# Moving weight casts and small vector work in a fused attention and star-ReLU kernel

## The chip, the cores and the metric

The kernel runs on one core of a Trainium2 chip. The metric is the device time of one execution in microseconds (us). Before the change it is 718.2 us, the median of three runs (718.13 to 718.25). The profile is of one execution of 718.1 us, in which the first and the last instruction are 716.3 us apart, at a granted TensorE clock of 0.997.

Engines are called as the profile calls them: PE is TensorE (PEld its weight loads), ACT is ScalarE, DVE is VectorE, POOL is GpSimd, SP is SyncE. POOL and SP issue transfers here (as does ACT at the start and the end).

## The reference, cut to what matters

There are two parts. The first is an attention across channels, for each of four batches of 6080 rows and 256 channels; the second is a feed-forward layer with 2048 hidden features over all 24320 rows.

```python
def _attn_ref(q, k, v, tau):
    qn = q / (np.linalg.norm(q, axis=1, keepdims=True) + 1e-06)
    kn = k / (np.linalg.norm(k, axis=1, keepdims=True) + 1e-06)
    s = kn.transpose(0, 2, 1) @ qn / tau        # 256 x 256 for each batch
    s = s - s.max(-1, keepdims=True)
    a = np.exp(s)
    a /= a.sum(-1, keepdims=True) + 1e-09
    return (v @ a).astype(np.float32)

def _moe_ref(x, w_in, w_out, s, b):             # x: the attention's output
    h = x @ w_in
    r = np.maximum(h, 0.0)
    g = s * (r * r) + b
    return (g @ w_out).astype(np.float32)
```

## The kernel before

The kernel folds the small matrix `a` into `w_in` once for a batch (`wa`), so that v times `wa` gives h at once. The rows are worked on in 48 groups of at most 512 (the last has 256). Each group has 16 **steps**, numbered through the program (step 16 is the first of group 1); in each step PE computes one block of 128 of the 2048 features (`mm1`). A pair of steps fills one of two PSUM tiles, which ACT reads out with a relu; squares of the results are taken by ACT or DVE.

The second product, g times `w_out`, is done one group later. In group 0 and the last group it is done plainly with `w_out16`. In all other groups it is done with seven products of half size instead of eight. For that DVE forms four sums of quarters of g (`S[1]` to `S[4]`), and w_out has to be combined once into `T1`, `T2`, `T3` and `N4`. The products are accumulated in three PSUM halves X, Y and Z, and DVE reads results out between them:

```python
products = [
    ("X", G(0, 0), W[:, 0, :, lo], p1),      # p1: DVE reads X into u1
    ("Z", lambda: S[1], T1, p5),             # p5: DVE reads Z into u5
    ("X", lambda: S[2], T2, p6),             # p6: DVE reads X into u2
    ("Y", G(1, 0), W[:, 1, :, lo], p2),
    ("X", lambda: S[3], T3, p7),
    ("Z", lambda: S[4], W[:, 1, :, hi], p3),
    ("X", G(1, 1), N4, p4),
]
# each product: 8 blocks x 2 matmuls of 128 columns; 7 of the 112 matmuls in each step,
# from step 3 of the next group on
```

So group 1's products begin at step 35. The third, which reads T2, takes the matmuls 32 to 47 (steps 39 to 41), the fifth, which reads T3, the matmuls 64 to 79 (steps 44 to 46). T2 and T3 are made in four pieces of two blocks each.

w_out is loaded in float32 in four pieces (`w_pieces`) and then worked on between the steps:

```python
def combine_w(i, k):                 # all on DVE, two pieces at a time
    for n in (2 * k, 2 * k + 1):
        for p in (2 * i, 2 * i + 1):
            ...
            if n == 0:   po(nc.vector.tensor_sub(T1[:, part, :], B12, B11))
            elif n == 1: po(nc.vector.tensor_sub(B12, B22, B12))      # what T3 is cast from
            elif n == 2: po(nc.vector.tensor_add(B11, B11, B12))      # what T2 is cast from
            else:        po(nc.vector.tensor_sub(N4[:, part, :], B21, B11))

def cast_w_out(i):                   # piece 0 on DVE, the others on ACT
    ...

def cast_w(T, i):
    w = w_pieces[i].rearrange("p (i h) c -> p h i c", h=2)
    po(nc.scalar.copy(out=T[:, ts(i, 2), :], in_=w[:, 0, :, :P] if T is T2 else w[:, 0, :, P:]))

CO = (7, 14, 18, 24)      # steps of cast_w_out
CW = (17, 20, 25, 27)     # steps of combine_w
CT = (32, 34, 36, 38)     # steps of cast_w for T2; for T3 six steps later
```

`po` keeps the order of the program on each engine. Work put on a step with `at_step` comes after the step's matmuls, relus, squares and sums. The pieces of w_out lie in the pool of eight buffers that the loads of q and k use too.

While a batch is worked on, the matrix and the norms of the next batch are prepared. Its q and k come in 12 chunks of 512 rows. For each chunk PE accumulates q by k (`s_ps`), and the squares for the norms are taken and folded into one block of rows:

```python
def norm_ops(self, c):
    # ops in this order, for batches 1 to 3:
    #   squares of k (ACT), squares of q (DVE), fold 4 -> 2 (DVE), fold 2 -> 1 (DVE),
    #   for chunks 1 to 10: a POOL transfer that adds the result to the first chunk's
    ...

def norm_step(gr=gr, c=c, sc=sc):    # sc: the step of the chunk's first matmuls
    ops = gr.norm_ops(c)
    for i, f in enumerate(ops):
        at_step(int(sc) + 2 + 1 + i * 3, f)
```

In batch 1, chunk 0 has sc = 26 and chunk 1 has 32.75.

The order of a step, with the squares of g and the sums S:

```python
SQUARES = {3: (0, 1, nc.scalar), 5: (1, 2, nc.scalar), 8: (2, 4, nc.vector),
           12: (4, 6, nc.vector)}
SUMS = {2: 1, 3: 2, 6: 3, 10: 4}

for s in range(NS + FT):
    g, m = divmod(s, FT)
    if g < NG:
        mm1(g, m)
    ...                                # seven matmuls of the products, and their p1 to p7
    if g < NG and m % 2 == 1:
        relu(g, m // 2)                # ACT
    ...
    if g < NG and g not in plain and m in SQUARES:
        square(g, *SQUARES[m])
    ...
    elif m == 0 and 0 < g and g - 1 not in plain:
        square(g - 1, 6, 8, nc.vector)
    elif 0 < g and g - 1 not in plain and m in SUMS:
        sums_of(g - 1, SUMS[m])        # DVE
    for f in side.pop(s, []):          # what at_step has put here
        f()
```

Of the kernel before, what the change touches and what calls it, by code (L numbers as in the profile page):

```python
# [17 lines left out]
def kernel(  # L18
# [12 lines left out]
    nc = tc.nc  # L31
    P = 128
# [14 lines left out]
    FT = Dff // P  # L47
    TG = 512
    NG = (NT + TG - 1) // TG
# [6 lines left out]
    def po(ins):  # L56

        tc.keep_in_program_order(ins)
        return ins
# [29 lines left out]
    T1, T2, T3, N4 = (wpool.tile([P, NP, P], FP16, name=n) for n in ("T1", "T2", "T3", "N4"))  # L89
# [287 lines left out]
    def group(g):  # L377
        t0 = g * TG
        return t0, min(TG, NT - t0) // P
# [3 lines left out]
    def load_v(g):  # L383
        t0, nj = group(g)
        v16 = vpool.tile([P, TG // P, C], FP16, tag="v16", name="v16")
        po(nc.gpsimd.dma_start(  # L386
            out=v16[:, :nj, :],
            in_=v_flat[t0 : t0 + nj * P, :].rearrange("(p j) c -> p j c", j=nj)))
        v_tiles[g] = v16

    def transpose_v(g):
        _, nj = group(g)
        v16 = v_tiles.pop(g)
        vT_ps = ps_o.tile([P, CH, TG], FP16, tag="o_ps", name="vT_ps")
        for j in range(nj):
            for ch in range(CH):
                po(nc.tensor.transpose(vT_ps[:, ch, ts(j, P)], v16[:, j, ts(ch, P)], ident16))
        vT = vtpool.tile([P, CH, TG], FP16, tag="vT", name="vT")
        po(nc.vector.tensor_copy(out=vT[:, :, : nj * P], in_=vT_ps[:, :, : nj * P]))
        vT_tiles[g] = vT  # L400

    def crossbar_v(g):

        _, nj = group(g)
        v16 = v_tiles.pop(g)
        vT = vtpool.tile([P, CH, TG], FP16, tag="vT", name="vT")
        for j in range(nj):
            po(nc.sync.dma_start_transpose(out=vT[:, :, ts(j, P)], in_=v16[:, j, :]))
        vT_tiles[g] = vT
# [74 lines left out]
    for c in range(NCH0 - NLATE):  # L484
        ops = g0.norm_ops(c)
# [3 lines left out]
        if c == NCH0 - NLATE - 1:  # L489
            ops, last_sum = ops[:-1], ops[-1]  # L490
# [4 lines left out]
    ops = {c: g0.norm_ops(c) for c in late}  # L495
# [40 lines left out]
    def combine_w(i, k):  # L536

        for n in (2 * k, 2 * k + 1):
            for p in (2 * i, 2 * i + 1):
                w = w_pieces[p].rearrange("p (i h) c -> p h i c", h=2)  # L540
                B11, B12 = w[:, 0, :, :P], w[:, 0, :, P:]
                B21, B22 = w[:, 1, :, :P], w[:, 1, :, P:]
                part = ts(p, 2)
                if n == 0:
                    po(nc.vector.tensor_sub(T1[:, part, :], B12, B11))
                elif n == 1:
                    po(nc.vector.tensor_sub(B12, B22, B12))
                elif n == 2:
                    po(nc.vector.tensor_add(B11, B11, B12))
                else:  # L550
                    po(nc.vector.tensor_sub(N4[:, part, :], B21, B11))

    def cast_w_out(i):
        if i == 0:
            po(nc.vector.tensor_copy(out=w_out16[:, ts(i, 4), :], in_=w_pieces[i]))
        else:
            po(nc.scalar.copy(out=w_out16[:, ts(i, 4), :], in_=w_pieces[i]))

    def cast_w(T, i):
        w = w_pieces[i].rearrange("p (i h) c -> p h i c", h=2)  # L560
        po(nc.scalar.copy(out=T[:, ts(i, 2), :], in_=w[:, 0, :, :P] if T is T2 else w[:, 0, :, P:]))


    side, early = {}, {}
# [1 line left out]
    def at_step(s, f):  # L566
        side.setdefault(int(s), []).append(f)
# [5 lines left out]
    for i, f in enumerate(folds):  # L573
        early.setdefault(FOLDS[i], []).append(f)
    at_step(14, lambda: po(nc.vector.tensor_scalar_mul(
        out=s_out, in0=s_bc, scalar1=1.0 / (LAM * LAM))))

    RC = (13, 16, 19, 21, 23)
    CO = (7, 14, 18, 24)
    CW = (17, 20, 25, 27)  # L580
    CT = (32, 34, 36, 38)
    for i in range(NPIECE):
        at_step(CO[i], lambda i=i: cast_w_out(i))
    for i in range(NPIECE + 1):
        at_step(RC[i], lambda i=i: rowconst_sum(i))
    at_step(30, rowconst_mm)
    for i in range(NPIECE):
        at_step(CW[i], lambda i=i: combine_w(i // 2, i % 2))
        at_step(CT[i], lambda i=i: cast_w(T2, i))
        at_step(CT[i] + 6, lambda i=i: cast_w(T3, i))  # L590
    for g in range(NG):
        if g >= 3:
            at_step(max(g - 4, 0) * FT + 2, lambda g=g: load_v(g))
        if g >= 1:
            if g == 1:
                at_step(12, lambda g=g: transpose_v(g))
            else:
                at_step((g - 2) * FT + 6, lambda g=g: crossbar_v(g))
    for b in range(1, B):
        gr = grams[b]  # L600
        w0 = first_group[b - 1] * FT + (26 if b == 1 else 6)
        w1 = first_group[b] * FT - 3
        NCH = len(gr.chunks)
        fin_len = 54
        span = (w1 - fin_len) - w0 - 12
        n = NCH * JC
        for c in range(NCH):
            sc = w0 + span * c * JC / n
            at_step(max(3, sc - 16), lambda gr=gr, c=c: gr.load(c))
            if c == 0:  # L610
                at_step(sc, gr.start)
            for j in range(JC):
                at_step(w0 + span * (c * JC + j) / n, lambda gr=gr, c=c, j=j: gr.mm(c, j))

            def norm_step(gr=gr, c=c, sc=sc):
                ops = gr.norm_ops(c)
                for i, f in enumerate(ops):
                    at_step(int(sc) + 2 + 1 + i * 3, f)
            at_step(sc + 1, norm_step)

        def fin_step(gr=gr, s=w1 - fin_len):
            ops = gr.finish_ops()
            for i, f in enumerate(ops):
                at_step(int(s) + 1 + (FIN[i] if i < len(FIN) else FIN[-1] + 3 * (i - len(FIN) + 1)), f)
        at_step(w1 - fin_len - 12, fin_step)
# [37 lines left out]
    def relu(g, i):  # L663
        n = group(g)[1] * P
        if i % 2 == 0:
            r_tiles[g, i // 2] = rpool.tile([P, 2, 2, TG], FP16, tag="r16", name="r16")
        r16 = r_tiles[g, i // 2]
        po(nc.scalar.activation(out=r16[:, :, i % 2, :n], in_=h_tiles.pop((g, i))[:, :, :n],  # L668
                                func=AF.Relu))

    def square(g, i0, i1, engine):

        n = group(g)[1] * P
        if i0 == 0:
            g_tiles[g] = gpool.tile([P, 2, NP, TG], FP16, tag="g16", name="g16")
        src = r_tiles[g, i0 // 2][:, :, i0 % 2 : i0 % 2 + i1 - i0, :n]
        dst = g_tiles[g][:, :, i0:i1, :n]
        if engine is nc.scalar:
            po(nc.scalar.activation(out=dst, in_=src, func=AF.Square))  # L679
        else:  # L680
            po(nc.vector.tensor_mul(dst, src, src))  # L681
# [79 lines left out]
    def seven_items(g):  # L761
# [56 lines left out]
        for n, (name, a, w, after) in enumerate(products):  # L818
            for i in range(NP):
# [15 lines left out]
    plain = {0, NG - 1}  # L835
    PLAG = {0: 11, NG - 1: 5}

    SQUARES = {3: (0, 1, nc.scalar), 5: (1, 2, nc.scalar), 8: (2, 4, nc.vector),
               12: (4, 6, nc.vector)}
# [10 lines left out]
# [4 lines that stand above are left out]
        for f in early.pop(s, []):  # L854
            f()

        if m == SHIFT and 0 < g and g - 1 not in plain:
            items = seven_items(g - 1)
            work.append((items, 8 if g == NG - 1 else 7))
        if work:  # L860
            items, n = work[0]
            for f in items[:n]:
                f()
            del items[:n]
            if not items:
                work.pop(0)
        for gp in plain:
            for mp in range(FT):
                if s == gp * FT + PLAG[gp] + (mp * 4 // 3 if gp == 0 else mp):
                    plain_mm2(gp, mp)  # L870
        if g < NG and m % 2 == 1:
            relu(g, m // 2)
            if g in plain:
                late = g > 0 and m // 2 % 2 == 0
                square(g, m // 2, m // 2 + 1, nc.scalar if late else nc.vector)
        if g < NG and g not in plain and m in SQUARES:
            square(g, *SQUARES[m])
        if g == NG - 1 and m in LAST:
            LAST[m]()
        elif m == 0 and 0 < g and g - 1 not in plain:  # L880
            square(g - 1, 6, 8, nc.vector)
        elif 0 < g and g - 1 not in plain and m in SUMS:
            sums_of(g - 1, SUMS[m])
        for f in side.pop(s, []):
            f()
# [34 lines left out]
```

## Time and profile before

| | us |
|---|---|
| time, median of 3 | 718.2 |
| span of the profiled run | 716.3 |
| PE busy in the span | 696.8 |
| DVE busy | 624.0 |
| ACT busy | 544.7 |
| POOL busy | 110.8 |
| ACT casts of T2 and T3 (8, mean of one) | 0.412 |
| ACT casts of w_out (3, mean of one) | 1.045 |
| ACT squares of a chunk's k (median of one) | 1.04 |
| DVE square of a chunk's q (mean of one, near 60 us) | 0.683 |
| DVE folds (mean of one, first and second) | 0.682 and 0.416 |

Durations of neighbouring instructions of one engine overlap in the profile, so the table's durations cannot simply be added: the distance from one start to the next is what an instruction takes of its engine. Ends of matmuls are modelled; their starts are recorded. In the profile's rows, "out<-in" gives the names of what is written and read, L with a number is the line of the kernel, x with a number counts instructions, and what stands in brackets is idle time of the engine before the instruction, with what ended it.

### The profile page before, as it was taken

Reading aid. Unit: us, or ns where it says so; the run is one execution under the profiler, and the core shown is the slowest. Engines: PE = TensorE matmul, PEld = TensorE weight load, DVE = VectorE, ACT = ScalarE, POOL = GpSimd, SP = SyncE. Lnnn points to the kernel's source line nnn. Section 1 sums busy time; section 2 is a strip of 40 time slices with the busy share of each in tenths; the row PEclk is TensorE's granted clock in tenths of the full one; section 3 lists DMA queues with packets and bytes.
Section 4 is the critical chain, followed back from the end, with each engine's and each line's share of the span. In section 5 each row is a group of like instructions: output and inputs, shape, how many; then the busy total and the mean of one; then the engine's idle time right before and its main releaser. Section 6 shows DMA issues by size and latency. Waiting matters only on the chain.

```text
span 716.3 us, 17491 instructions
## 1 busy us (share of the span) xinstructions
PE 696.8 (97%) x7421; PEld 503.6 (70%) x7421; DVE 624.0 (87%) x877; ACT 544.7 (76%) x592; POOL 110.8 (15%) x189
## 2 busy tenths in 40 slices
PE   4699999999999999999999999999999999999998
PEld 2456777776677777777677777777668777777777
DVE  4889999988789989998889899998887888888886
ACT  5779877787777777778777778777877777777874
POOL 4532332102101222101010222110000000000000
PEclk9999999999999999999999999999999999999999
DMA  9999999636565978444672887843323333321201
GB/s 236 207 259 167 165 174 136 122 89 124 111 122 109 135 134 144 112 89 95 138 146 52 145 137 125 153 90 77 98 63 75 94 70 75 97 60 46 82 31 75
DMA packets 87454, 83.47 MB, mean 117 GB/s; under 512 B 56304, under 2 KB 62256, under 8 KB 87376
## 3 DMA queue, kind: packets, MB, share of 16 engines
q0 software_dynamic: 26608, 43.40, 37.7%
q1 hardware_dynamic: 60192, 37.64, 22.0%
q8 instruction: 58, 0.95, 0.6%
q10 hardware_dynamic: 576, 1.31, 0.5%
q14 instruction: 20, 0.16, 0.1%
HBM read 78.91 MB, written 24.90 MB: 145 GB/s over the span
## 4 chain that ended last, share of the span: by engine, by line
PE 93%; DMA 3%; DVE 2%; ACT 2%; issue 0%; ACTq 0%; DVEq 0%
PE h_ps L658 45%; PE o_ps L826 40%; PE s_ps L148 4%; PE wa_ps L327 2%; DMA qk<-in_k_dram 1%; DMA raw<-in_q_dram 1%; ACT sq L177 1%; PE o_ps L730 1%; DVE f L191 1%; PE o_ps L704 0%; ACT r L668 0%; ACT r L269 0%; DVE sq L174 0%; PE n_ps L244 0%; DVE o_sb L686 0%
## 5 line engine op out<-in xcount | busy, mean ns | idle before, releaser
L668 ACT ACTIVATE r<-h_ps 128x1024 f16<-128x1024 f32 (+1 forms) x384 | 388.4, 1013 | 151.8 <-PE h_ps L658 148.1
L658 PE MATMUL h_ps<-vT,wa 128*128 128x512 f16 (+7 forms) x1632 | 452.2, 364 | 0.6 <-ACT wa L320 0.5
L826 PEld LDWEIGHTS <-S 128*128 128x128 f16 x2944 | 198.0, 98 | 84.8 <-issue 0.2
L826 PEld LDWEIGHTS <-g 128*128 128x128 f16 x2208 | 155.1, 98 | 74.1
L681 DVE TENSOR_TENSOR g<-r 128x2048 f16<-128x2048 f16 (+2 forms) x150 | 174.6, 1164 | 14.0 <-ACT r L668 13.6
L826 PE MATMUL o_ps<-T,S 128*128 128x128 f16 x2208 | 183.3, 219 | 0.1
L658 PEld LDWEIGHTS <-wa 128*128 128x128 f16 x1632 | 135.8, 98 | 20.6 <-ACT wa L320 0.8
L826 PE MATMUL o_ps<-w_out,g 128*128 128x128 f16 x1472 | 134.2, 219 | 0.2 <-DVE u L686 0.2
L686 DVE SCALAR_TENSOR_TENSOR o_sb<-o_ps,s_out,u 128x256 f32<-128x256 f32 x138 | 66.4, 481 | 50.9 <-PE o_ps L826 48.8
L679 ACT ACTIVATE g<-r 128x1024 f16<-128x1024 f16 (+1 forms) x97 | 100.4, 1035 | 0.2
L148 PE MATMUL s_ps<-qk 128*128 128x256 f16 (+1 forms) x384 | 71.7, 288 | 14.2 <-ACT qk L139 9.0
L386 POOL DMA_DIRECT2D v<-in_v_dram x48 | 31.0, 648 | 263.6 <-DMA vT<-v 187.0
L686 DVE SCALAR_TENSOR_TENSOR u<-o_ps,s_out,rowconst 128x256 f32<-128x256 f32 x138 | 65.8, 477 | 0.0
L826 PE MATMUL o_ps<-w_out,S 128*128 128x128 f16 x736 | 63.5, 219 | 0.0
L826 PE MATMUL o_ps<-N,g 128*128 128x128 f16 x736 | 63.4, 219 | 0.0
L207 POOL DMA_DIRECT2D f<-f x30 | 26.3, 876 | 224.3 <-DVE f L191 183.1
L755 DVE TENSOR_TENSOR S<-S,g 128x2048 f16<-128x2048 f16 (+1 forms) x47 | 56.4, 1201 | 1.3
L177 ACT ACTIVATE sq<-qk 128x1024 f16<-128x1024 f16 (+2 forms) x53 | 54.5, 1041 | 3.9 <-DMA qk<-in_k_dram 2.3
L753 DVE TENSOR_TENSOR S<-g 128x2048 f16<-128x2048 f16 (+1 forms) x47 | 56.0, 1192 | 0.0
L757 DVE TENSOR_TENSOR S<-g 128x2048 f16<-128x2048 f16 x46 | 55.9, 1215 | 0.0
L759 DVE TENSOR_TENSOR S<-g,S 128x2048 f16<-128x2048 f16 x46 | 55.8, 1214 | 0.0
L148 PEld LDWEIGHTS <-qk 128*128 128x128 f16 (+1 forms) x384 | 33.0, 103 | 20.8 <-ACT qk L139 9.5
(83 smaller groups left out, 313.9 us busy)
## 6 DMA issues: line engine op xcount, KB each, us to landing
out_dram<-o_sb SPq DMA_DIRECT2D x42, 512.0 KB, 2.9
v<-in_v_dram POOLq DMA_DIRECT2D x47, 256.0 KB, 4.9
qk<-in_k_dram POOLq DMA_DIRECT2D x42, 256.0 KB, 7.0
qk<-in_q_dram POOLq DMA_DIRECT2D x42, 256.0 KB, 7.7
f<-f POOLq DMA_DIRECT2D x30, 128.0 KB, 3.1
vT<-v SPq DMA_TRANSPOSE x182, 3.0
out_dram<-o_sb SPq DMA_DIRECT2D x10, 256.0 KB, 5.4
w<-in_moe_w_out_dram POOLq DMA_DIRECT2D x4, 512.0 KB, 10.1
```

Of the source, the lines that this page charges most:

```text
L148: po(nc.tensor.matmul(self.s_ps[:, ch, :], qc[:np_, j, ts(ch, P)], kc[:np_, j, :], start=(c == 0 and j == 0 and ch == 0), stop=(c == len(s ...
L177: po(nc.scalar.activation(out=st["sq"][:np_, a, js, :], in_=(qc, kc)[a][:np_, js, :], func=AF.Square))
L658: po(nc.tensor.matmul(dst, wa[:, ci, ts(m, P)], src, start=(ci == 0), stop=(ci == CH - 1), skip_group_check=True))
L668: po(nc.scalar.activation(out=r16[:, :, i % 2, :n], in_=h_tiles.pop((g, i))[:, :, :n], func=AF.Relu))
L679: po(nc.scalar.activation(out=dst, in_=src, func=AF.Square))
L681: po(nc.vector.tensor_mul(dst, src, src))
L686: po(nc.vector.scalar_tensor_tensor(out=dst, in0=src, scalar=s_out, op0=ALU.mult, in1=add, op1=ALU.add))
L753: po(nc.vector.tensor_add(T[1], A21, A22))
L755: po(nc.vector.tensor_sub(T[2], T[1], A11))
L757: po(nc.vector.tensor_sub(T[3], A11, A21))
L759: po(nc.vector.tensor_sub(T[4], A12, T[2]))
L826: po(nc.tensor.matmul(st[name][:, j, :], a()[:, i, ts(j, P)], w[:, i, :], start=first, stop=last, skip_group_check=True))
```

## The change: what it does and what it is for

- **w_out's casts (CO)**: the casts of pieces 1, 2 and 3 into `w_out16` are put on steps 12, 14 and 18.
- **T2 and T3 (cast_w, CT)**: the eight casts are no longer ACT instructions, but transfers from SBUF to SBUF, issued by GpSimd, that convert float32 to float16 on the way. T2's pieces are put on steps 22, 23, 28 and 29, T3's two steps later each. This is to take work from ACT in a part of the program that is rich in such side work.
- **NORM_STEPS and the rule after it**: the squares and folds of chunks 0 and 1 of batch 1 get steps of their own. For all other chunks of batches 1 to 3, a start at the fourth step of a group is put off by three steps, and a first fold on steps 12 or 13 of a group goes to step 14. This is to keep them from standing ahead of what PE waits for.
- **squares**: in group 1, the second of the two squares that ACT takes goes from the sixth step of the group to the eighth.

```diff
     def cast_w(T, i):
         w = w_pieces[i].rearrange("p (i h) c -> p h i c", h=2)
-        po(nc.scalar.copy(out=T[:, ts(i, 2), :], in_=w[:, 0, :, :P] if T is T2 else w[:, 0, :, P:]))
+        po(nc.gpsimd.dma_start(out=T[:, ts(i, 2), :], in_=w[:, 0, :, :P] if T is T2 else w[:, 0, :, P:]))
 ...
-    CO = (7, 14, 18, 24)
+    CO = (7, 12, 14, 18)
     CW = (17, 20, 25, 27)
-    CT = (32, 34, 36, 38)
+    CT = (22, 23, 28, 29)
 ...
         at_step(CT[i], lambda i=i: cast_w(T2, i))
-        at_step(CT[i] + 6, lambda i=i: cast_w(T3, i))
+        at_step(CT[i] + 2, lambda i=i: cast_w(T3, i))
 ...
+    NORM_STEPS = {(1, 0): (29, 32, 38, 39), (1, 1): (38, 41, 44, 47, 50)}
 ...
                 ops = gr.norm_ops(c)
-                for i, f in enumerate(ops):
-                    at_step(int(sc) + 2 + 1 + i * 3, f)
+                at = NORM_STEPS.get((gr.b, c))
+                if at is None:
+                    s0 = int(sc) + 3
+                    if s0 % FT == 3:
+                        s0 += 3
+                    s2 = s0 + 6
+                    if s2 % FT in (12, 13):
+                        s2 += 14 - s2 % FT
+                    at = (s0, s0 + 3, s2, s2 + 3, s2 + 6)
+                for s, f in zip(at, ops):
+                    at_step(s, f)
 ...
-        if g < NG and g not in plain and m in SQUARES:
-            square(g, *SQUARES[m])
+        squares = {**SQUARES, 5: (), 7: SQUARES[5]} if g == 1 else SQUARES
+        if g < NG and g not in plain and squares.get(m):
+            square(g, *squares[m])
```

## The prediction

> **What bounds the kernel now.** I first read how busy each engine is (busy us, share of the span, instructions) and the shares of the chain of waits.
>
> ```profile
> PE 696.8 (97%) x7421; PEld 503.6 (70%) x7421; DVE 624.0 (87%) x877; ACT 544.7 (76%) x592; POOL 110.8 (15%) x189
> ...
> PE 93%; DMA 3%; DVE 2%; ACT 2%; issue 0%; ACTq 0%; DVEq 0%
> ```
>
> TensorE (PE) bounds the program. The change leaves every matmul in place, so it can only take away moments in which PE is held up. A busy PE in the stage table does not show these: a matmul that starts late seems to run longer. So I read the start times in PE's timeline and compare distances. Undisturbed, two 512-column matmuls take 0.43 us to the next start, four of 256 columns 0.43 to 0.44, two of 256 columns 0.22, seven of 128 columns 0.39 (0.056 each). The first stretch in which distances are longer (start, us, engine, line, operation):
>
> ```profile
> 54.30 1.03 PE L658 MATMUL h_ps<-vT,wa 128*128 128x512 f16 x4
> 55.16 0.60 PE L730 MATMUL o_ps<-w_out,g 128*128 128x256 f16 x4
> 55.82 0.59 PE L658 MATMUL h_ps<-vT,wa 128*128 128x512 f16 x2
> ...
> 57.12 0.60 PE L730 MATMUL o_ps<-w_out,g 128*128 128x256 f16 x4
> 57.68 0.59 PE L658 MATMUL h_ps<-vT,wa 128*128 128x512 f16 x2
> ...
> 59.19 0.38 PE L148 MATMUL s_ps<-qk 128*128 128x256 f16 x2
> 59.53 0.59 PE L658 MATMUL h_ps<-vT,wa 128*128 128x512 f16 x2
> ```
>
> From 55.16 to 55.82 is 0.66, so 0.22 lost; 57.12 to 57.68 loses 0.12, 59.19 to 59.53 another 0.12. Each time a product h waits for its PSUM buffer, that is for ScalarE (ACT) to finish the relu of two pairs before: ACT is busy 4.97 of 5.00 us from 51 to 56 and 4.00 of 4.00 from 56 to 60. The second stretch, on PE, VectorE (DVE) and ACT:
>
> ```profile
> 69.33 0.79 PE L826 MATMUL o_ps<-T,S 128*128 128x128 f16 x7
> 69.96 0.38 PE L148 MATMUL s_ps<-qk 128*128 128x256 f16 x2
> ...
> 71.43 0.62 PE L826 MATMUL o_ps<-T,S 128*128 128x128 f16 x6
> 72.25 0.22 PE L826 MATMUL o_ps<-w_out,g 128*128 128x128 f16 x1 [0.21 <-DVE u L686]
> ```
>
> ```profile
> 68.66 0.68 DVE L191 TENSOR_TENSOR f<-sq 128x1024 f16<-128x1024 f16 x1
> 69.26 0.48 DVE L686 SCALAR_TENSOR_TENSOR u<-o_ps,s_out,rowconst 128x256 f32<-128x256 f32 x1
> 69.66 1.22 DVE L757 TENSOR_TENSOR S<-g 128x2048 f16<-128x2048 f16 x1
> 70.79 0.42 DVE L191 TENSOR_TENSOR f<-f 128x512 f16<-128x512 f16 x1
> 71.12 0.68 DVE L174 TENSOR_TENSOR sq<-qk 128x1024 f16<-128x1024 f16 x1
> 71.73 0.47 DVE L686 SCALAR_TENSOR_TENSOR u<-o_ps,s_out,rowconst 128x256 f32<-128x256 f32 x1
> ```
>
> ```profile
> 70.90 0.71 ACT L561 CAST T<-w 128x256 f16<-128x256 f32 x2
> ```
>
> From 69.33 to 69.96 is 0.63 where 0.39 is due: 0.24 lost, because the third product cannot use its PSUM bank before the first u is read out of it (done at 69.74), and a fold of q and k sits right before that u. From 71.43 to 72.25 is 0.82 where 6 x 0.056 = 0.34 is due: 0.48 lost. About 0.12 of it is the third product's fifteenth column block waiting for the last piece of T2, cast by ACT until 71.61; about 0.37 is the fourth product waiting for the second u (done 72.21), which stands behind a fold and a square. A further 0.06 follows at 72.59. This stretch loses 0.79 us (0.24 + 0.12 + 0.37 + 0.06, each rounded).
>
> In the rest of the timeline, I find only short hold-ups of this kind: 0.07 before 139.28, 0.12 before 247.52, 0.17 before 262.43, 0.12 before 420.18, 0.17 before 435.09, 0.14 before 703.46. All that PE loses from 55 us on is then 0.47 + 0.79 + 0.79 = about 2.05 us of 718. The loss in the first 44 us (loads, norms of the first batch) is not touched by the change. **So no outcome can gain more than about 0.3%.**
>
> [...] every casting load (qk, v, w_in) stands on POOL. [...] The 128 KB transfers f<-f of this trace took 2.7/3.1/7.0 us (min, median, max), so 3 us and more is the figure to use, and crowded queues more than double it. [...] from 60 to 64 us DVE is busy 3.89 of 4.00 us and POOL issues loads 0.52 us apart, each 0.53 to 0.58 long. [...] a cast of T lasts 0.41 us, but the next ACT instruction starts 0.30 us after it (68.74 to 69.04). I therefore count start to start.
>
> **The change part by part.**
>
> 1. *T2 and T3 by GpSimd transfers.* Eight ACT casts leave (8 x 0.30 = 2.4 us of ACT between 63.9 and 76.2), eight POOL issues come. Only the cast that ends at 71.61 held PE: 0.12 us off the path, the rest was beside other work.
>
> 2. *w_out's casts at steps 7, 12, 14, 18 instead of 7, 14, 18, 24.* By counting two h matmuls a step, step 12 starts at 46.0, step 18 at 51.26, step 24 at 55.82. ACT idles 1.11 us before its relu at 47.95, and a cast takes 0.92 there, so the cast moved to step 12 costs nothing (its piece must have landed: issued at 35.2, 10.1 us to landing). The cast at 57.50 goes. A cast at step 18 (51.95) stays, with another piece.
>
> 3. *Group 1's second ACT square from step 21 to 23.* It ran at 55.65, ahead of the relu at 56.59; now the relu comes first. Parts 2 and 3 free the relus that PE waited for at 57.68 and 59.53: 0.12 + 0.12 = 0.25 us (unrounded) off. The wait at 55.82 is for the relu that ends at 55.76; before it come relu, cast (step 18), relu, square, relu, none of which the change removes, so its 0.22 stays.
>
> 4. *Steps of chunks 0 and 1 of batch 1.* The first fold goes from step 35 to 38, the second from 38 to 39, and chunk 1's squares and folds three steps later. DVE's order becomes u, S, fold, u, fold. The first u ends 0.60 us earlier (69.14 against 69.74), PE wants it at about 69.55; the second u loses the 0.33 and 0.60 before it and ends near 71.3 against 72.21, PE wants it near 71.8. So 0.24 + 0.37 + 0.06 = 0.67 us off.
>
> 5. *Other chunks.* Where a chunk's squares began at the fourth step of a group they begin three later: chunk 6 of batches 2 and 3 goes from steps 243 and 435 to 246 and 438. Its ACT square at 258.56 is what put the relus behind at 262.43 and 435.09: 0.35 us off. A first fold at the group's steps 12 or 13 goes to step 14: the fold at 138.15 was ahead of the read-out that PE waited for at 139.28: 0.07 off. The waits at 247.52 and 420.18 come from chunk 4, whose steps stay: 0.24 stays, as does 0.14 at the end.
>
> Sum: 0.12 + 0.25 + 0.67 + 0.35 + 0.07 = 1.46 us, so 716.7 us if nothing new waits.
>
> **Rivals.** *(a) A late transfer in place of a late cast.* In its order POOL gets to the casts only after the load of v at step 18, which it issued at 59.00 (idle 9.05 us before it). Behind it come casts and loads in the order of steps. With 0.52 us a load and an estimated 0.71 a cast (of the loads in the trace w's took longest, 0.75, and w_in's 0.71), the last piece of T2 is issued at 59.0 + 3 x 0.52 + 5 x 0.71 = 64.1 and the last of T3 at 64.1 + 2 x 0.71 + 2 x 0.52 = 66.6. VectorE has combined the later pieces by 61.5. PE needs them at about 71.05 (71.66 less the 0.61 saved before) and 75.2 (step 46 at 76.3 less 1.05). With the 3.1 us of f<-f they land at 67.2 and 69.7, with the 8.5 us of the q loads between 42 and 80 us at 72.6 and 75.1. The queue is full there (DMA share 1.01 to 1.19 from 60 to 72 us). The hardware queue's packets take 0.22 x 716.3 x 16 / 60192 = 0.042 us each; 16 such rows a DMA engine is 0.7 us a cast, an estimate, over 5 us for all eight, which pushes q and k loads back too. For these: the waits would be 0 to 1.5 us, cancelling the gain. Against: small transfers have a margin of up to 4 us, and loads of later chunks need no longer wait for w's buffers (POOL waited 3.6 us for a T cast). Time if so: 717.2 to 718.5.
>
> *(b) VectorE is the bound anyway.* DVE is busy 4.00 of 4.00 us from 68 to 72, and the change takes nothing from it; folds put off come back at steps 38 to 50 and may hold other read-outs. For it: little slack. Against: PE had none of these waits from 73 to 139 at 96% busy DVE. Time if so: 717.0 to 717.8.
>
> *(c) Hidden anyway.* If PE's shortest path after a freed wait runs into the next one, only half of the 1.46 counts: 717.5.
>
> **Range and chances.** I take 716.7 and add about 0.35 for (a) and 0.05 for (b): 717.1 us. The low end, 716.4, is everything removed and the 0.22 at 55.82 as well; the high end, 718.4, is (a) at its worst. A change over 2% would be 14 us: the gain is capped at 2 us, and a loss of that size would need a stall that nothing here suggests. Same 0.98, faster 0.01, slower 0.01.
>
> **What would show it.** Step 1: eight POOL transfers T<-w, no ACT casts of T, and no late start of T,S matmuls; a PE wait on such a transfer would make (a) true. Steps 2 and 3: starts 0.43 apart between 57 and 60, and 0.66 remaining at the place of 55.16. Step 4: 0.39 for the seven T,S matmuls, no wait for u. Step 5: 0.33 less at two places, with 247.52 and 420.18 keeping their 0.12. The prediction is wrong if PE waits appear between 69 and 77 us for T or for qk, or if the start before 44 us shifts.

## The result, and the profile after

The changed kernel takes **720.89 us** (median of six runs, 719.28 to 723.51), the kernel before 718.13 us (six runs, 718.05 to 718.25). The ratio is 1.0043, with a 95% interval of 1.0025 to 1.0061: slower by 0.4%, where I had predicted a gain of 0.15%. The spread from run to run grew from 0.2 us to 4.2 us. The profiled run is the longest of the six (723.5 us, span 721.7), so its waits must be larger than those of a median run.

The rows of the page after that answer to those of before (busy us, share of the span, instructions; then the shares of the chain of waits, by engine):

```profile
PE 698.4 (97%) x7421; PEld 504.2 (70%) x7421; DVE 624.2 (86%) x877; ACT 542.9 (75%) x584; POOL 117.0 (16%) x197
...
PE 89%; DMA 4%; DVE 4%; ACT 2%; issue 1%; POOL 0%; DVEq 0%; ACTq 0%
```

Eight instructions have gone from ACT to POOL, as meant. PE still fills 97% of a longer span; only the chain has moved, 4% of it from PE to transfers, DVE and issue. Most of the loss is seen in one place, in PE's timeline after (start, us, engine, line, operation, and in brackets what ended the idle time before it):

```profile
69.23 0.55 PE L836 MATMUL o_ps<-T,S 128*128 128x128 f16 x7
70.23 0.39 PE L148 MATMUL s_ps<-qk 128*128 128x256 f16 x2 [0.45 <-DMA qk<-in_q_dram]
70.46 0.59 PE L668 MATMUL h_ps<-vT,wa 128*128 128x512 f16 x2
70.89 0.44 PE L836 MATMUL o_ps<-T,S 128*128 128x128 f16 x5
74.45 0.33 PE L836 MATMUL o_ps<-T,S 128*128 128x128 f16 x2 [3.11 <-DMA T<-w]
74.58 1.06 PE L668 MATMUL h_ps<-vT,wa 128*128 128x512 f16 x2
75.43 0.42 PE L836 MATMUL o_ps<-T,S 128*128 128x128 f16 x2
76.30 0.58 PE L836 MATMUL o_ps<-T,S 128*128 128x128 f16 x4 [0.46 <-DMA T<-w]
```

Distances tell: 0.61 us lost before 70.23, for q of chunk 2; 3.28 before 74.45, for the third piece of T2; 0.76 before 76.30, for its fourth. The two h matmuls at 74.58 then take 0.85 us to the next start in place of 0.43: after the long wait the granted clock is 0.50 of full speed from 75.0 to 77.5 us and 1.00 again from 78.0; in the table by stages that is 0.82 on average from 72 to 76 us and 0.76 from 76 to 80. By the starts from 74.45 to 78.01, that costs another 1.2 us. The same stretch in the trace before lost 0.79 us.

The transfers themselves, in the view of the tile T (the row of POOL's issues, and the last line of the view):

```profile
L561 POOL DMA_DIRECT2D T<-w x8: 706/750/767, 59.5 to 70.5; - x8
...
DMA to landing us min/median/max: 4.0/9.7/12.6
```

Issues last 0.71 to 0.77 us and began at 59.5, as I had worked out. But from issue to landing a cast takes **9.7 us in the middle and 12.6 at most**, where I had reckoned with 3.1 to 8.5. T2's last two pieces, issued at 63.4 and 64.1, took 11.0 and 12.2 us: they landed at 74.4 and 76.3.

### The profile page after: what moved, and what is told of

Its sections match the earlier page's. It is cut to its first block, busy times and chain, and to the rows that moved or that the text cites. A ratio compares the mean times of both kernels' runs of the same rounds, so it can differ in the third digit from the quotient of the medians.

```text
span 721.7 us, 17504 instructions
## 1 busy us (share of the span) xinstructions
PE 698.4 (97%) x7421; PEld 504.2 (70%) x7421; DVE 624.2 (86%) x877; ACT 542.9 (75%) x584; POOL 117.0 (16%) x197
## 4 chain that ended last, share of the span: by engine, by line
PE 89%; DMA 4%; DVE 4%; ACT 2%; issue 1%; POOL 0%; DVEq 0%; ACTq 0%
PE h_ps L668 43%; PE o_ps L836 39%; PE s_ps L148 4%; PE wa_ps L327 2%; DMA T<-w 2%; DMA qk<-in_k_dram 1%; DMA raw<-in_q_dram 1%; ACT sq L177 1%; DVE f L191 1%; DVE g L691 1%; PE o_ps L714 0%; DVE acc L526 0%; ACT r L269 0%; DVE S L763 0%; POOL T L561 0%
## 5 line engine op out<-in xcount | busy, mean ns | idle before, releaser
L836 PE MATMUL o_ps<-N,g 128*128 128x128 f16 x736 | 63.4, 219 | 0.0
```

The lines of the kernel that those rows point to most:

```text
L836: po(nc.tensor.matmul(st[name][:, j, :], a()[:, i, ts(j, P)], w[:, i, :], start=first, stop=last, skip_group_check=True))
```

## The experiments

All times are medians. The kernel before, run beside them, took 718.13 us for the changed kernel, 718.15 for the next four rows, 718.21 for "store later", "T2 ahead of T3", "no rule" and "steps by the waits", and 718.23 for the other three. Waits and landings are read from one profiled run of each kernel.

| run | time, us | ratio to before, 95% interval |
|---|---|---|
| changed kernel | 720.89 | 1.0043 (1.0025 to 1.0061) |
| casts on ACT again | 718.27 | 1.0002 (0.9994 to 1.0010) |
| before, with transfers only | 721.03 | 1.0041 (1.0027 to 1.0054) |
| load of v later | 717.70 | 0.9995 (0.9987 to 1.0004) |
| transposes at step 46 | 722.21 | 1.0060 (1.0046 to 1.0073) |
| store later | 723.35 | 1.0070 (1.0055 to 1.0084) |
| T2 ahead of T3 | 722.38 | 1.0056 (1.0040 to 1.0071) |
| fifth buffer for v | 717.58 | 0.9991 (0.9983 to 1.0000) |
| transposes behind a store | 718.50 | 1.0007 (0.9998 to 1.0016) |
| load of v later, no rule | 717.19 | 0.9988 (0.9982 to 0.9995) |
| load of v later, steps by the waits | 716.36 | 0.9973 (0.9963 to 0.9984) |
| the same, casts on ACT | 718.01 | 0.9997 (0.9988 to 1.0005) |

### Is it the transfers?

Two runs: the casts undone, and the casts alone.

```diff
 # casts on ACT again (from the changed kernel)
-po(nc.gpsimd.dma_start(out=T[:, ts(i, 2), :], in_=...))
+po(nc.scalar.copy(out=T[:, ts(i, 2), :], in_=...))
-CT = (22, 23, 28, 29)      # and T3 at CT + 2
+CT = (32, 34, 36, 38)      # and T3 at CT + 6
```

> The changed kernel with the eight casts of T2 and T3 on ScalarE again, at the steps of before; everything else stays changed. Theory A (the transfers land late, and nothing else costs): the 3.3, 0.7 and 0.6 us waits near 70 to 76 us and the slow matmuls after them go, the time is 717.3 to 717.8: before (718.1) less 0.25 (relus near 58 us) less 0.67 (read-outs near 70 us) plus 0.2 to 0.5 for new short waits near 280 and 453 us. Theory B (the moved squares and folds cost): it stays at 719 or more.

```diff
 # before, with transfers only
-po(nc.scalar.copy(out=T[:, ts(i, 2), :], in_=...))
+po(nc.gpsimd.dma_start(out=T[:, ts(i, 2), :], in_=...))
-CT = (32, 34, 36, 38)      # and T3 at CT + 6
+CT = (22, 23, 28, 29)      # and T3 at CT + 2
```

> The kernel before with one thing changed: T2 and T3 cast by GpSimd transfers at the new steps. Theory A: as slow as the changed kernel or slower, 719.5 to 724, with PE waiting for T<-w after the third product's eighth column block, spread over more than 1 us from run to run. Theory B: within 0.4 us of before.

The casts alone make the kernel before as slow as the changed one (721.03 us); PE waits 3.7 us for T in three places there. Without them the changed kernel is level with before (718.27), not 0.3 to 0.8 us faster as I expected. The rest of that expectation went into a new wait, in PE's timeline of the run with the casts on ACT:

```profile
71.83 0.38 PE L148 MATMUL s_ps<-qk 128*128 128x256 f16 x2
72.75 0.59 PE L668 MATMUL h_ps<-vT,wa 128*128 128x512 f16 x2 [0.54 <-ACT r L678]
```

From 71.83 to 72.75 is 0.92 in place of 0.22: 0.70 us lost to a relu. In ACT's timeline, two casts (70.11) and chunk 1's square (70.71, moved to step 38 by the change) stand ahead of the relu at 71.67. So the schedule of the change and the transfers belong together: the moved square needs the place that the casts leave.

### Why do they land late: GpSimd's order, or what else is moving?

POOL's timeline after shows what the casts stand behind:

```profile
58.97 0.53 POOL L386 DMA_DIRECT2D v<-in_v_dram  x1 [9.03 <-DMA vT<-v]
59.50 1.42 POOL L561 DMA_DIRECT2D T<-w  x2
60.91 0.56 POOL L132 DMA_DIRECT2D qk<-in_k_dram  x1
61.45 0.58 POOL L132 DMA_DIRECT2D qk<-in_q_dram  x1
61.98 3.57 POOL L561 DMA_DIRECT2D T<-w  x5
```

GpSimd had issued everything ahead of it by 50 us, and then stood for 9.03 us before the load of v for group 5, which is ahead of the casts in its order, until transposes had landed: that load takes a buffer of v that earlier transposes still read. I tested the hold in two ways. First, that load behind the casts:

```diff
 # load of v later
-at_step(max(g - 4, 0) * FT + 2, lambda g=g: load_v(g))
+at_step(32 if g == 5 else max(g - 4, 0) * FT + 2, lambda g=g: load_v(g))
```

> The changed kernel, but the load of v for group 5 goes from step 18 to step 32, behind the casts in GpSimd's order. If the casts are late because GpSimd stands 9 us before that load (its order), the first casts are issued near 57 us in place of 59.5, the later T2 pieces near 61.7 in place of 63.4, and land before 71 us: 717.3 to 718. If they are late because the transfer queues are crowded whatever the order, T2's last pieces still land after 73 us and the time stays between 719 and 723.

Second, the order left as it is, and only the reason for the hold taken away:

```diff
 # fifth buffer for v
-vpool = pool("vpool", 4)
+vpool = pool("vpool", 5)
```

> The changed kernel with five buffers for v in place of four and no other edit: the load of v for group 5 then has a buffer that nothing reads, and does not hold GpSimd until group 2's transposes have landed (58.4 us); the order in the queue is the same. If that hold is the cause, the load is issued near 50 us, the first casts near 55.7, T2's last piece near 61.3, landed before 70 us: 717.3 to 718.0. If the 512 KB of that load ahead of the casts were the cause, it stays above 719.

Both came out: 717.70 and 717.58 us. With the fifth buffer the load stays ahead of the casts, but is issued 9 us earlier, so this run by itself does not tell the hold from the load's own bytes. The trace of the changed kernel does: there the load landed 4.4 us after its issue, at 63.4 us, when T2's last two pieces were only being issued. So its own bytes were through by then, and what is left of the two is the hold. POOL's timeline and the landings (view of T) with the fifth buffer:

```profile
49.98 0.54 POOL L386 DMA_DIRECT2D v<-in_v_dram  x1
55.83 1.42 POOL L561 DMA_DIRECT2D T<-w  x2 [5.31 <-DVE w L549]
...
DMA to landing us min/median/max: 3.8/4.6/8.7
```

The casts are now held by DVE, which combines the pieces, and issued 3.7 us earlier. They also land faster once issued, 4.6 us against 9.7, and PE has no wait for T or qk in this stretch. So a late issue is not all. Four runs asked what slows the transfers that are issued late. First, the transposes of v for group 4, which SyncE issues from 65.05 us on:

```diff
 # transposes at step 46
-at_step((g - 2) * FT + 6, lambda g=g: crossbar_v(g))
+at_step(46 if g == 4 else (g - 2) * FT + 6, lambda g=g: crossbar_v(g))
```

> The changed kernel, but the transposing transfers of v for group 4 go from step 38 to step 46, so that the hardware queue has only one store between 64 and 78 us. If those transposes are what slows the casts' packets, T2's last pieces land by 72 us and the time is 717.3 to 718.5. If they only share the time, nothing changes: 719 to 723.

It took 722.21 us, and tells nothing of the transposes: SyncE's timeline shows them issued at 64.86, as before:

```profile
64.86 6.55 SPq L408 DMA_TRANSPOSE vT<-v  x4
```

No store of SyncE came between the old step and the new one, so the later step moved nothing. At step 49 one does (the edit is the same with 49 for 46):

> The changed kernel with the transposes of v for group 4 put behind a store of group 1 in SyncE's order (step 49), so that they are truly issued after 78 us (at step 46 they stood behind no store, and SyncE issued them at 64.9 us as before). If the hardware queue's transposes are what stretches the casts' transfers, T2's last piece lands by 71.5 us: 717.5 to 718.5 us. If not, PE waits for T<-w until 73 us or later: 719.5 to 723.

In SyncE's timeline of this run the transposes start at 80.06 us:

```profile
80.06 6.10 SPq L408 DMA_TRANSPOSE vT<-v  x4
```

The time is 718.50, against 720.89: **the transposes matter too**. All casts but the last are issued when they were in the changed kernel, but land sooner; T2's last two pieces take 7.8 and 7.5 us. The view of T, then the row of PE's waits for them (us in total, times, longest):

```profile
L561 POOL DMA_DIRECT2D T<-w x8: 703/750/767, 59.5 to 69.0; - x8
...
DMA to landing us min/median/max: 4.1/7.3/7.8
```

```profile
PE o_ps L836 <- DMA T<-w: 0.3, 1, 0.3
```

A landing of 7.8 us at most lies in the range that I had assumed, and the wait is 0.3 us, 0.46 by distances. The other two runs looked for the cause elsewhere, and neither gained time. In one, the 512 KB store of group 0 waits:

```diff
 # store later (in plain_mm2)
-store(g)
+at_step(44, lambda: store(g)) if g == 0 else store(g)
```

> The changed kernel, but the 512 KB store of group 0 (issued at 64.6 us) is put off to step 44. If that store is what the last pieces of T2 share the transfer engines with, they land 1.5 to 3 us earlier, by 72.5 us, and the time falls to 718 to 719.5. If what stands ahead of them in GpSimd's own queue is the cause, it stays at 720 to 722.

723.35 us. The store was issued at 69.5 us in place of 64.6, but SyncE issued the transposes 2.2 us earlier instead, at 62.9, so the run does not test the store alone. T2's last two pieces still took 10.5 and 10.6 us. The run with the transposes behind a store says more: there the store of group 0 was issued at 64.79, and no piece took over 7.8 us, so the store without the transposes does not bring the loss. In the other, T3's casts stand behind T2's:

```diff
 # T2 ahead of T3
-at_step(CT[i] + 2, lambda i=i: cast_w(T3, i))
+at_step(30 + i, lambda i=i: cast_w(T3, i))
```

> The changed kernel with T3's casts behind T2's (steps 30 to 33 in place of 24, 25, 30, 31), so that two casts fewer stand ahead of T2's last two pieces and they are issued 1.4 us earlier, at 62.0 and 62.7 us. If the queue works in order and every cast ahead costs, they land 1.5 to 3 us earlier, at 71.5 to 73.5, and the time is 718.5 to 720; T3's last piece then lands near 78 us and may be waited for instead, by up to 1 us. If the casts cost nothing to each other: 720 to 722 as before.

722.38 us. T2's last piece was issued 1.4 us earlier and landed 1.6 us earlier, at 74.7 us, still 11.9 us after its issue; PE needs it near 71, and then waited another 0.75 us for T3. So the casts ahead cost the time of their issue and little more. Of what I tried, only an end to the hold or the transposes out of the way brought T2 there nearly in time.

### The steps of the other chunks, and what is left to gain

```diff
 # load of v later, no rule (from the kernel with the load of v later)
 s0 = int(sc) + 3
-if s0 % FT == 3:
-    s0 += 3
 s2 = s0 + 6
-if s2 % FT in (12, 13):
-    s2 += 14 - s2 % FT
```

> The kernel with the load of v for group 5 at step 32, and without the change's rule for the squares and folds of the other chunks (chunks 0 and 1 of batch 1 keep their new steps). From the two traces: the two 0.24 us waits near 274 and 447 us go, the 0.07 us wait near 139 us comes back, the ones near 246, 261, 419 and 434 us stay: 0.40 us less than the 717.7 us with the rule, 717.3. If the rule does what it was meant to do: 718 or more.

717.19 us, as the two traces said: the rule costs 0.4 to 0.5 us. DVE's timeline of the changed kernel shows how, and contradicts my prediction:

```profile
275.99 0.42 DVE L191 TENSOR_TENSOR f<-f 128x512 f16<-128x512 f16 x1
...
279.11 0.69 DVE L191 TENSOR_TENSOR f<-sq 128x1024 f16<-128x1024 f16 x1
279.71 0.48 DVE L696 SCALAR_TENSOR_TENSOR u<-o_ps,s_out,rowconst 128x256 f32<-128x256 f32 x1
```

The rule puts chunk 6's second fold (275.99) at the second step of a group. DVE then works without a gap (a read-out and two sums S, in place of the dots, and chunk 7's fold) up to the u at 279.71, so u is 0.33 us later, and PE loses 0.24 there and 0.24 again at 453 us.

The last two runs begin with this kernel. In the first, I chose steps by the waits that were left:

```diff
 # load of v later, steps by the waits
-NORM_STEPS = {(1, 0): (29, 32, 38, 39), (1, 1): (38, 41, 44, 47, 50)}
+NORM_STEPS = {(1, 0): (29, 37, 39, 40), (1, 1): (38, 41, 44, 47, 50),
+              (1, 11): (103, 106, 110, 113)}
+for b, s in ((2, 0), (3, 192)):
+    NORM_STEPS[b, 4] = tuple(s + x for x in (224, 227, 231, 233, 236))
+    NORM_STEPS[b, 6] = tuple(s + x for x in (249, 246, 252, 255, 258))
-squares = {**SQUARES, 5: (), 7: SQUARES[5]} if g == 1 else SQUARES
+squares = {**SQUARES, 3: (), 5: SQUARES[3], 7: SQUARES[5]} if g == 1 else SQUARES
```

> The same without the rule, and with steps chosen by the waits that are left: group 1's two ScalarE squares at its steps 5 and 7 (0.22 us at 55.7), chunk 0's square of q at step 37 (0.07 at 67.2), chunk 4's first fold of batches 2 and 3 one step later (2 x 0.12), the ScalarE square of chunk 6 of these batches at step 9 of the group, behind both squares of g (2 x 0.18), and chunk 11's folds of batch 1 at 110 and 113 (0.07). If each wait is on the path alone: 717.3 less 0.95, 716.3 to 716.6. If PE only meets the next wait: 717 or more.

716.36 us, as each wait alone had promised, and faster than both kernels. In the second its casts are on ACT again:

> The fastest version so far (716.36 us) with the eight casts back on ScalarE at their old steps. If the transfers are worth something when they land in time, the 0.7 us wait for a relu near 72.7 us is back and the time is 716.9 to 717.2; if ScalarE has room for them, 716.3 to 716.5.

718.01 us. I expected one relu wait of 0.7 us; PE's timeline shows 0.79 before 72.80, 0.68 before 63.66 and 0.33 before 79.66, together 1.80. So when they land in time, the eight transfers are worth 1.65 us on this schedule. Its other steps were chosen with the transfers in place; what a schedule chosen for casts on ACT could reach is not tested.

## Why the prediction was wrong

- **Parts 2 and 3 (relus near 58 us): right.** In PE's timeline after, the starts at 57.17, 57.61, 58.04 and 59.13 have their undisturbed distances, and only the 0.22 before 55.88 is left.
- **Part 4 (u near 70 us): right.** No wait for u is left there; 0.08 us is new at the first matmul with T1 (67.47).
- **Part 5: wrong for chunk 6, right for chunk 11.** The wait at 139 us is gone. Those of 262 and 435 us are still there (0.17 each): I took it that moving chunk 6's ACT square by three steps takes it out of the relus' way, but it only goes from behind the first square of g to behind the second, still ahead of the same relu. At step 9 of the group it was out of the way: in the run with steps by the waits, PE's distance at that place (260.93 to 260.99) is an undisturbed 0.06. And the rule's cost on DVE, 0.47, I did not look for: expected 0.42 off, got 0.40 on.
- **Part 1: the step that failed.** The cast on ACT was worth 0.12 on the path, and its replacement became the wait of rival (a), for which I allowed 0 to 1.5 us. The mechanism of (a) was named, and T2's issue times were right (the last of T3 came at 70.5 us, not 66.6). The term mis-sized was the time to landing: put at 3.1 to 8.5 us, it was 11.0 and 12.2 for T2's last two pieces, and PE lost 5.85 us near 74 us in the profiled run (0.61 + 3.28 + 0.76, and 1.2 of slow clock). Both my figures were medians, the lower of the transfers f<-f, the first of which is issued at 78 us, the upper of the loads of q over 38 us. What I set against (a) failed too: loads of k and q, which I thought freed of a wait for T, waited 2.8 us in three places for T's transfers. The trace before held a better figure: of the two loads of v that GpSimd issued between 58.9 and 64 us, where the casts would go, the slower took 11.1 us to land.

```profile
L386 POOL DMA_DIRECT2D v<-in_v_dram x2: 528/552/576, 59.0 to 61.6; - x2
...
DMA to landing us min/median/max: 3.9/7.5/11.1
```

- I also took landings as fixed. The six runs of the changed kernel lie 1.7 to 5.9 us above the 717.58 of the kernel with a fifth buffer, so the wait seems to vary from run to run (only one of the six has a trace). A single figure for the landing could not have given a range that holds them.
- **The clock** was in no part. Its 1.2 us is a fifth of what the profiled run lost near 74 us.

The sum for the profiled run, from starts: 0.61 + 3.28 + 0.76 + 1.2 for T, q and the clock, 0.47 for the rule, 0.08 at 67.47, less 1.11 saved (0.25 near 58, 0.79 near 70, 0.07 at 139), is 5.3 us; the spans differ by 5.4.

Both the late issue and the transposes are needed for most of the loss: without the one it is 717.6 us, without the other 718.5. What the transposes do inside the transfer engines stays open. A cast ran beside them where it had time: with the load of v later, SyncE issued the transposes from 64.82 us on and GpSimd the last cast at 64.9; no cast took more than 7.7 us, and PE waited for none.

## What to carry to other kernels

Here, work that went from an engine to a transfer traded a duration that hardly varied (0.40 to 0.43 us for the ACT casts of before) for a landing that did (4.0 to 12.6 us after), so size such a move by the slowest landing in its own stretch, not by a median of the kernel. Before you put an instruction behind others in an engine's order, look for what that engine is already held by: one load that waited 9.03 us for a buffer held eight casts that had nothing to do with it. And look for what the engine does between the old step and the new one: with no store of SyncE in between the transposes were still issued at 64.86 us, behind one at 80.06.

## What I had not expected of the hardware

The granted clock fell after one long wait of PE and not after another of about the same length. One row of the table by stages (stretch and its us, then busy us and instructions of PE, PEld, DVE, ACT and POOL, the granted clock of PE, DMA share, GB/s), first of the changed kernel, then of the one with the store later:

```profile
72.00:76.00 4.00, 1.40 (x6) 0.68 (x6) 0.66 (x1) 0.27 (x1) 1.06 (x2) 0.82 1.61 103
```

```profile
72.00:76.00 4.00, 1.88 (x20) 1.37 (x20) 1.48 (x3) 1.08 (x2) 1.75 (x4) 1.00 1.41 167
```

In the first, a hold-up of 3.28 us by distances (3.11 us of idle time in the profile) ended at 74.45, and the clock was 0.82 in this stretch. In the second, the longest wait for T was 3.3 us of idle time, and the clock was 1.00. With the transposes at step 46, PE was busy 5.39 of 8.00 us from 68 to 76 us, and the clock was 0.67 from 72 to 76; in the kernel before with transfers only, PE was busy 5.44 of the same 8.00 us, and the clock was 1.00. So in these runs neither the length of a hold-up nor the busy share of PE told whether the clock fell; what decides is not shown.
